# A job list that counts DMA transfers one behind the other, three matmuls less at the start of banks, and a new order of splits under the last A V product

## The chip, the core and the metric

The kernel runs on one core of a Trainium2 chip. The metric is device time in microseconds (us) of one launch. The core has five engines, each of which takes its own instructions in program order: PE (TensorE: matrix products into the eight PSUM banks), DVE (VectorE), ACT (ScalarE), POOL (GpSimd) and SP (SyncE, which here does little but issue DMA transfers). They meet only through semaphores, so an instruction that waits holds up all that stands behind it on its engine.

## The reference, cut to what matters

```python
# q, k, v: (4, 12, 448, 64) float32
scores = np.matmul(q, k.transpose(0, 1, 3, 2)) / np.sqrt(64)     # causal mask, softmax over the last axis
x = np.matmul(softmax(scores), v)                                 # -> (4 * 448, 12 * 64) = (1792, 768)
h = x @ w_in                                                      # w_in (768, 2048)
g = np.maximum(h, 0.0) + alpha * np.minimum(h, 0.0)               # PReLU, alpha per column
out = g @ w_out                                                   # w_out (2048, 768) -> (1792, 768)
```

The two weight matrices arrive as 64-bit floats; the kernel makes 32-bit floats of them with integer operations on their halves.

## The kernel before, in words

**Attention.** The 24 pairs of heads (six for each of four batches) go through a software pipeline. A text table (`ORDER`) says for every round which step of which pair is emitted: scores (`S0`..`S2`), row maxima, exponentials, normalising on POOL (`NO`), transposes on PE (`PT`, L582), their copies out of PSUM (`C00`, `C10`, `C21`, ...: DVE L504, ACT L502), and the product with V (`AV`, L602). Other work hangs on steps of single pairs by hooks (`after(pair, step, function)`).

**Both layers of the MLP** are block products with seven products in place of eight. The steps are called P1, P5, P6, P2, P7, P3, P4; each reads one block or sum of blocks of the left side (A11, S1, S2, A12, S3, S4, A22) and one of the right side (B11, T1, T2, B21, T3, B22, T4) and writes a bank in the role Y, V, X or Z. After P1, ACT copies bank Y to bank X (`fork`; L402 in the first layer, L1371 in the second). After P5, ACT copies bank V to SBUF (`keep`; L406, L1376). After P6 DVE or ACT makes bank Z from Y and the kept V (`Z`, L409; `oz` in the second layer, L1383 or L1275), and P7 and P3 wait for that. Each operand is split into a high and a low part: ACT rounds a copy (the cast, "hi"), DVE or POOL subtracts it from the operand ("lo"), and PE multiplies hi by hi, lo by hi and hi by lo. A step therefore waits for the "lo" of both its operands.

**First layer.** `h_step` (matmuls on L395, nine of 128x448 to a step) runs groups g = 0..7 of `w_in`, for the two halves b = 0, 1 of the tokens. Group 0 of half 0 runs between the last steps of attention. Half 1 needs the splits of its x blocks T1, T2, T3, T4, B21, B22 (ACT `x2_hi`, L849; DVE `x2_lo`, L853). B22 and two thirds of B21 come back from DRAM by DMA (`x2l_B<-xd_B`); the last third of B21 and T4 are what the last `AV` completes. `FIRST` is the order of the steps of group 0 for half 1. The results go through ACT `relu` (L419), DVE `act` (L423) and a store (L429) to DRAM (`gd`). A "piece" is 768 KB of a 64-bit weight matrix: loaded by SP (L278, L283), then ACT L296 and L300, POOL L304, DVE L308 and L312, POOL L318; pieces of `w_out` are stored to DRAM (`wd`, L323).

**Second layer.** Four quarters Q of `w_out`, each for seven row tiles, are 28 tiles q, taken in 14 pairs p; a step is six matmuls of 128x384 (L1262). For every pair SP loads g (`gl`, four transfers on L1210), and sums (L1230), casts (ACT L1236) and lows (L1240) follow. For every quarter SP loads weights (`wl`, L1178), and sums (DVE L1188), casts (ACT L1195, into a slot `w`) and lows (DVE L1199) follow. The quarter changes inside pair 3 (tile 6 is of quarter 0, tile 7 of quarter 1).

**What sets the order.** From the end of attention on, everything is a job of `Plan`. A job names its engine, a duration (table `US`), the jobs it comes after, the room (a buffer slot) that it takes and the ones it gives back, and a due time, which is worked back from the order of the steps on PE. `Plan.order` plays the list through when the program is built, starting on each idle engine the ready job with the earliest due time, and the instructions are emitted in the order of these starts. So the model of time in `Plan` sets only an order; on the chip each engine keeps that order and waits as it must. `busy["way"]` keeps POOL and the marked DVE operations from overlapping in the plan. In the kernel before, a load counts as landed 4.0 us after its issue and a store 3.0 us, however many others are under way.

`ready_bank` takes the next PSUM bank and runs one matmul of 128x448 on it (L803) whose result nothing uses.

## Time and profile before

| what | value |
|---|---|
| median of 3 runs | 586.35 us (584.92 to 589.84) |
| profiled execution | 589.1 us, its span 587.3 us, so 1.8 us around the span |
| PE busy | 572.3 us, 97% of the span |
| DVE, ACT, POOL busy | 473.6 (81%), 390.0 (66%), 294.0 us (50%) |
| mean granted clock of PE | 0.993 |
| chain that ended last | 84% PE, 7% DVE, 4% DMA |

Span is from the first to the last instruction of the profiled execution. A busy share is the time in which an engine had an instruction under way. The granted clock is a share of full speed: 1.0 is 2.4 GHz and 0.5 is 1.2 GHz. The chain that ended last is followed back from the last instruction to what released each one. In a timeline, the bracket at the end of a line is the idle time of the engine just ahead of it and what ended it. "x1l", "gset" and so on in the rows are buffers; "bank" is any PSUM bank.

### The profile page before, as it was taken

The numbers are of one execution on the slowest core, as the hardware profiler recorded it, in microseconds if no ns is written. First come the engines' busy times: TensorE is split into PE (matmuls) and PEld (weight loads), VectorE is DVE, ScalarE is ACT, GpSimd is POOL, SyncE is SP. The second block draws the span as 40 slices with busy tenths as digits, with TensorE's granted clock in tenths as the row PEclk, the third lists the DMA queues.
The fourth block names the chain that finished last, engine by engine and source line by source line (L and its number), as shares of the span: only waits on it lengthen the run. The fifth ranks groups of instructions, "written<-read, shape, count | busy, mean of one in ns | idle before, by whom it ended". The sixth has DMA issues, their size and how long they took to land.

```text
span 587.3 us, 10245 instructions
## 1 busy us (share of the span) xinstructions
PE 572.3 (97%) x3300; PEld 498.2 (85%) x3300; DVE 473.6 (81%) x993; ACT 390.0 (66%) x898; POOL 294.0 (50%) x340
## 2 busy tenths in 40 slices
PE   8999999999998999999999999989989999999997
PEld 4666676666877999999999998989879999999997
DVE  5998998899779687687678779858989888879963
ACT  6989897999676566665656636667756656555431
POOL 7766687875624433544445414224525552645530
PEclk9999999999998999999999999989999999999999
DMA  6876546321336575766767564873352414403532
GB/s 167 211 149 172 136 127 178 113 65 63 89 139 217 182 252 203 255 221 222 266 216 251 166 216 148 262 239 127 99 153 77 140 42 148 133 10 119 179 108 108
DMA packets 82981, 93.48 MB, mean 159 GB/s; under 512 B 11632, under 2 KB 72016, under 8 KB 82928
## 3 DMA queue, kind: packets, MB, share of 16 engines
q1 hardware_dynamic: 82032, 91.19, 49.8%
q0 software_dynamic: 576, 1.18, 0.8%
q8 instruction: 26, 0.43, 0.3%
q10 hardware_dynamic: 320, 0.46, 0.3%
q14 instruction: 27, 0.22, 0.1%
HBM read 64.50 MB, written 28.31 MB: 158 GB/s over the span
## 4 chain that ended last, share of the span: by engine, by line
PE 84%; DVE 7%; DMA 4%; issue 2%; ACT 2%; SPq 1%; POOL 0%; DVEq 0%; ACTq 0%; POOLq 0%
PE bank L395 31%; PE bank L1262 27%; PE bank L602 8%; PE bank L582 7%; PE bank L525 6%; PE bank L517 4%; DMA tf<-gd 2%; DMA gd<-tf 2%; DVE dec L1188 1%; DVE x1l L1240 1%; DVE x1h L1199 1%; PE bank L445 1%; DVE tf L423 1%; SPq L1210 0%; DMA wd<-acc 0%
## 5 line engine op out<-in xcount | busy, mean ns | idle before, releaser
L506 POOL TENSOR_SCALAR p<-p,rs 128x128 f32<-128x128 f32 (+3 forms) x164 | 84.3, 533 | 34.9 <-DVE rs L563 17.1
L552 ACT ACTIVATE p<-bank,nm 128x256 f32<-128x256 f32 (+3 forms) x168 | 82.5, 507 | 14.0 <-DVE nm L537 11.2
L1262 PE MATMUL bank<-x1h,x1l 128*128 128x384 f32 x444 | 81.9, 335 | 1.3 <-DVE x1h L1199 1.3
L1262 PEld LDWEIGHTS bank<-x1h,x1l 128*128 128x128 f32 x444 | 77.8, 188 | 1.6 <-DVE x1h L1199 1.5
L537 DVE CUSTOM_DVE_ANT_0 bank<-bank,mask 128x128 f32<-128x128 f32 (+3 forms) x168 | 71.0, 480 | 9.7 <-PE bank L525 5.6
L419 ACT ACTIVATE tf<-bank 128x448 f32<-128x448 f32 x64 | 34.1, 542 | 35.0 <-PE bank L395 21.3
L582 PEld LDWEIGHTS bank<-ident,p 128*128 128x128 f32 x384 | 43.3, 141 | 12.0 <-issue 7.8
L423 DVE SCALAR_TENSOR_TENSOR tf<-tf,om,bank 128x448 f32<-128x448 f32 x64 | 41.4, 673 | 13.3 <-ACT tf L419 13.2
L602 PEld LDWEIGHTS bank<-ptf,v 128*64 128x64 f32 x384 | 25.4, 136 | 30.8 <-issue 13.0
L582 PE MATMUL bank<-ident,p 128*128 128x128 f32 x384 | 47.2, 274 | 0.9 <-POOL p L506 0.8
L1262 PE MATMUL bank<-x1h,gset 128*128 128x384 f32 x228 | 45.1, 348 | 2.5 <-ACT bank L1371 1.8
L602 PE MATMUL bank<-ptf,v 128*64 128x448 f32 (+3 forms) x384 | 46.8, 386 | 0.0
L395 PE MATMUL bank<-x1h,wir 128*128 128x448 f32 x192 | 44.7, 368 | 0.5 <-DVE bank L409 0.5
L1262 PEld LDWEIGHTS bank<-x1h,gset 128*128 128x128 f32 x228 | 41.5, 195 | 3.4 <-ACT bank L1371 2.2
L318 POOL TENSOR_TENSOR dec<-dec,tf 128x768 int32<-128x768 int32 x13 | 26.3, 2020 | 33.4 <-ACT tf L419 13.7
L525 PE MATMUL bank<-kr,qr 64*128 64x384 f32 (+2 forms) x288 | 41.0, 397 | 0.0
L395 PEld LDWEIGHTS bank<-x1h,wir 128*128 128x128 f32 x192 | 35.9, 188 | 4.1 <-DVE bank L409 0.8
L502 ACT ACTIVATE ptf<-bank 128x512 f32<-128x512 f32 (+1 forms) x71 | 38.0, 583 | 1.7 <-PE bank L582 1.7
L1262 PE MATMUL bank<-wo,x1l 128*128 128x384 f32 x186 | 35.7, 339 | 1.1 <-DVE wo L1199 1.1
L552 ACT ACTIVATION_READ_ACCUMULATOR p<-bank,nm 128x1 f32 x168 | 35.9, 214 | 0.0
L1262 PEld LDWEIGHTS bank<-wo,x1l 128*128 128x128 f32 x186 | 32.9, 188 | 1.5 <-DVE wo L1199 1.5
L409 DVE TENSOR_TENSOR bank<-bank,tf 128x448 f32<-128x448 f32 x30 | 18.9, 629 | 18.6 <-PE bank L395 18.4
(190 smaller groups left out, 1383.2 us busy)
## 6 DMA issues: line engine op xcount, KB each, us to landing
gd<-tf SPq DMA_DIRECT2D x64, 224.0 KB, 2.0
tf<-gd SPq DMA_DIRECT2D x28, 256.0 KB, 4.4
acc<-gd SPq DMA_DIRECT2D x28, 256.0 KB, 4.4
dec<-in_moe_w_in_dram SPq DMA_DIRECT2D x9, 768.0 KB, 4.9
tf<-in_moe_w_in_dram SPq DMA_DIRECT2D x7, 768.0 KB, 4.6
dec<-in_moe_w_out_dram SPq DMA_DIRECT2D x7, 768.0 KB, 5.0
tf<-in_moe_w_out_dram SPq DMA_DIRECT2D x7, 768.0 KB, 4.3
dec<-wd SPq DMA_DIRECT2D x13, 384.0 KB, 4.5
```

The source lines that it names most:

```text
L318: nc.gpsimd.tensor_tensor(out=y, in0=y, in1=low, op=ALU.add)
L395: nc.tensor.matmul(ps, w[:, u, k * P : (k + 1) * P], x[:, k], start=(st in ("P1", "P5") and i == 0), stop=(i == len(mms) - 1), skip_group_ ...
L419: nc.scalar.activation(t, bank_of(g, b, role), AF.Relu, scale=-1.0)
L423: stt(out=t, in0=t, scalar=om[:, f : f + 1], in1=bank_of(g, b, role), op0=ALU.mult, op1=ALU.add)
L502: eng.activation(out, x, AF.Copy, scale=side)
L506: eng.tensor_scalar(out=out, in0=x, scalar1=side, scalar2=1.0, op0=ALU.mult, op1=ALU.mult)
L525: nc.tensor.matmul(ps[:, o : o + lim], T["q", p][half(j), i * QP : (i + 1) * QP], T["k", p][half(j), :lim], start=(o == 0), stop=(n > 0 or ...
L537: nc.vector.tensor_tensor_reduce(out=t, in0=t, in1=masks[1] if i == NQ else masks[0][:, (NQ - 1 - i) * QP :], scale=-SCALE, scalar=MOST_F3 ...
L552: nc.scalar.activation(T["p", p, i][:, j, : t.shape[1]], t, AF.Exp, scale=-1.0, bias=T.pop(("nm", p, i, j)), accum_out=T["sm", p][:, z : z ...
L582: nc.tensor.transpose(ps[:, j - js[0], c], t[:, j, c * QP : (c + 1) * QP], T["ident"])
L602: nc.tensor.matmul(out[half(j), c * QP :], vs[b % 2][:, hp, c, j], x[:, c * QP : S], start=(c == 0), stop=(c == NQ),)
L1262: nc.tensor.matmul(ps, x, w, start=(st in ("P1", "P5")[: 1 if Q else 2] and i == 0), stop=(i == len(mms) - 1), skip_group_check=True,)
```

## The change

- `Plan` knows a transfer's length (`move`, table `MOVE`): a transfer lands at the later of its issue plus 1.35 and the landing of the one before it, plus its own length. Loads with a due time are not issued earlier than 45 us ahead of it.
- Three of the four `ready_bank` matmuls go; the banks are taken as they are.
- `Z` of group 0, half 0, is hooked behind the copy `C00` instead of `C21` of the last pair, so it stands one copy earlier on DVE.
- T3's cast is emitted behind T1's and T2's, ahead of the last `AV`'s results; it is no job any more.
- In group 0 of half 1, P2 (which reads B21) runs ahead of P7 (T3) and P3 (B22); B21 is loaded ahead of B22.
- The casts of quarter weights keep the order of the steps (`wc_last`).

Left out of the diff: the parameter `move` itself, handed down by the other jobs that issue a transfer.

```diff
--- before.py
+++ after.py
@@ -60,13 +60,17 @@
...
+START, AHEAD = 1.35, 45.0
+MOVE = {"raw": 2.7, "piece": 1.4, "x": 0.9, "act": 0.62, "w": 0.95, "g": 1.05, "out": 0.7}
...
@@ -102,7 +106,9 @@
...
-        busy, events, now = {}, [], 0.0
+        busy, now, moved = {}, 0.0, 0.0
+        early = dict(then=[], next=[], give=[], n=-1)
+        events = [(j["by"] - AHEAD, 0, early) for j in self.jobs if j["move"] and AHEAD < j["by"] < 1e6]
...
@@ -119,6 +125,8 @@
...
+                    if j["move"] and j["lag"] == LOAD and now < j["by"] - AHEAD - 1e-6:
+                        continue
...
@@ -127,7 +135,10 @@
...
-                    events += [(now + us, 0, j), (now + us + j["lag"], 1, j)]
+                    end = now + us + j["lag"]
+                    if j["move"]:
+                        end = moved = max(moved, now + START) + j["move"]
+                    events += [(now + us, 0, j), (end, 1, j)]
...
@@ -170,7 +181,7 @@
...
 STEPS = ["P1", "P5", "P6", "P2", "P7", "P3", "P4"]
-FIRST = ["P1", "P5", "P6", "P7", "P3", "P2", "P4"]
+FIRST = ["P1", "P5", "P6", "P2", "P7", "P3", "P4"]
...
@@ -804,8 +815,7 @@
...
     def begin_block():
-        y, v_, x = ring.popleft(), ring.popleft(), ready_bank()
-        bk[0] = [y, v_, x, None]
+        bk[0] = [ring.popleft() for _ in range(3)]
         rooms["v"] = Slots([ap["low"].tile([P, S], F32, tag="low", name="low_v")])
         for st in ("P1", "P5"):
...
@@ -817,7 +827,7 @@
...
     def plus_z():
-        bk[0][3] = ready_bank()
+        bk[0].append(ring.popleft())
         h_plus(0, 0, "Z")
 
...
@@ -855,7 +865,7 @@
     def scores_over():
...
-        for nm in ("T1", "T2"):
+        for nm in ("T1", "T2", "T3"):
             x2_hi(nm, (0, KW))
...
@@ -908,7 +918,7 @@
...
         after(last - 1, "AV", go_on)
-        after(last, "C21", plus_z)
+        after(last, "C00", plus_z)
         after(last, "C30", last_of_it)
...
@@ -922,15 +932,15 @@
...
-        bk[1] = [ready_bank(), ready_bank(), ring.popleft(), ring.popleft()]
-        bk[1] = bk[1][2:] + bk[1][:2]
+        v_, z, y, x = ring.popleft(), ready_bank(), ring.popleft(), ring.popleft()
+        bk[1] = [y, v_, x, z]
...
-        done.add(("load", piece_names[3]))
+        done |= {("load", piece_names[3]), ("xh", "T3")}
...
@@ -980,7 +990,7 @@
...
-        PARTS = {"T3": (0, KW), "B22": (0, KW), "B21": (0, KW - 1), "T4": (0, KW)}
+        PARTS = {"T3": (0, KW), "B21": (0, KW - 1), "B22": (0, KW), "T4": (0, KW)}
...
@@ -989,11 +999,12 @@
...
-                job(("xh", nm), "ACT", f"cast{n}", lambda nm=nm, ks=ks: x2_hi(nm, ks), of)
+                if ("xh", nm) not in done:
+                    job(("xh", nm), "ACT", f"cast{n}", lambda nm=nm, ks=ks: x2_hi(nm, ks), of)
...
@@ -1287,7 +1298,7 @@
...
-                    dec_end + [("store", ("o", 4 * Q + c + 2 * u)) for u in range(2)], "wf", lag=LOAD, behind=list(wl_last),
+                    dec_end + [("store", ("o", 4 * Q + c + 2 * u)) for u in range(2)], "wf", lag=LOAD, behind=list(wl_last), move=MOVE["w"],
...
@@ -1308,7 +1319,8 @@
...
-                job(("wcast", Q, nm), "ACT", "wcast", lambda nm=nm: w_cast(Q, nm), of, "w")
+                job(("wcast", Q, nm), "ACT", "wcast", lambda nm=nm: w_cast(Q, nm), of, "w", behind=list(wc_last))
+                wc_last[:] = [("wcast", Q, nm)]
...
@@ -1322,7 +1334,7 @@
...
-                        lag=LOAD, behind=gl_last + ([] if first else [("gl", 2 * p, 0)]),
+                        lag=LOAD, move=MOVE["g"], behind=gl_last + ([] if first else [("gl", 2 * p, 0)]),
...
```

The new file is longer, so its lines have other numbers: what was L402, L406, L409, L419, L849, L853 is L413, L417, L420, L430, L859, L863, and what was L296, L1178, L1188, L1199, L1210, L1240 is L307, L1189, L1199, L1210, L1221, L1251.

ACT at the end of attention, before (`x2h_T` and `x2h_B` are casts of x blocks of half 1, `dec<-dec` a piece, L402 the fork and L406 the keep of half 1):

```order
L849 ACTIVATE x2h_T_2343<-tf 128x1344
L502 ACTIVATE x2h_B_2370<-bank_65 128x448
L849 ACTIVATE x2h_T_2345<-tf 128x1344
L296 ACTIVATE dec<-dec 128x768
L300 ACTIVATE dec<-dec 128x768
L849 ACTIVATE x2h_T_2366<-tf 128x1344
L402 ACTIVATE bank_64<-bank_68 128x448
L849 ACTIVATE x2h_B_2368<-x2l_B_2369 128x1344
L406 ACTIVATE tf<-bank_65 128x448
L849 ACTIVATE x2h_B_2370<-x2l_B_2371 128x896
L373 ACTIVATE wie<-dec 128x384
L419 ACTIVATE tf<-bank_63 128x448
```

and now:

```order
L859 ACTIVATE x2h_T_2341<-tf 128x1344
L859 ACTIVATE x2h_T_2343<-tf 128x1344
L513 ACTIVATE x2h_B_2369<-bank_65 128x448
L307 ACTIVATE dec<-dec 128x768
L311 ACTIVATE dec<-dec 128x768
L859 ACTIVATE x2h_T_2365<-tf 128x1344
L430 ACTIVATE tf<-bank_63 128x448
L859 ACTIVATE x2h_B_2369<-x2l_B_2370 128x896
L413 ACTIVATE bank_65<-bank_68 128x448
L384 ACTIVATE wie<-dec 128x384
L430 ACTIVATE tf<-bank_67 128x448
L417 ACTIVATE tf<-bank_64 128x448
```

T3's cast is third of three at the start; the cast of B21 (128x896) stands ahead of the fork (now L413), which stood ahead of both casts of B blocks; the cast of B22 comes behind the keep.

SP at the beginning of the second layer, before (`gd_87<-tf` stores the last results of the first layer, `acc<-gd` and `tf<-gd` load g for the pairs 1 and 2, `in_moe_w_out` is a piece):

```order
L1178 DMA wie<-wd 128x2x384
L429 DMA gd_87<-tf 128x448
L1178 DMA dec<-wd 128x2x384
L429 DMA gd_87<-tf 128x448
L1178 DMA dec<-wd 128x2x384
L283 DMA tf<-in_moe_w_out_dram 128x1536
L1210 DMA tf<-gd_84 128x4x128 x4
L1178 DMA dec<-wd 128x2x384
L323 DMA wd<-acc 128x768
```

and now:

```order
L1189 DMA wie<-wd 128x2x384
L440 DMA gd_87<-tf 128x448 x2
L1189 DMA dec<-wd 128x2x384
L440 DMA gd_87<-tf 128x448
L1221 DMA tf<-gd_84 128x4x128 x4
L1189 DMA dec<-wd 128x2x384 x2
L294 DMA tf<-in_moe_w_out_dram 128x1536
L334 DMA wd<-acc 128x768
L294 DMA acc<-in_moe_w_out_dram 128x1536
```

The load of g for pair 2 stood behind a piece and now stands ahead of it. On ACT, at the same place, before (L296 and L300 are that piece, L1236 casts of g, L1371 the forks of tiles 2 and 3):

```order
L296 ACTIVATE tf<-tf 128x768
L300 ACTIVATE tf<-tf 128x768
L1236 ACTIVATE x1l<-acc 128x512
L1371 ACTIVATE bank_62<-bank_63 128x384
L1236 ACTIVATE x1l<-acc 128x512
L1371 ACTIVATE bank_61<-bank_65 128x384
L1236 ACTIVATE x1l<-tf 128x512
L1376 ACTIVATE acc<-bank_67 128x384
```

and now:

```order
L1383 ACTIVATE bank_62<-bank_63 128x384
L1247 ACTIVATE x1l<-acc 128x512
L1383 ACTIVATE bank_61<-bank_64 128x384
L1247 ACTIVATE x1l<-tf 128x512
L1388 ACTIVATE acc<-bank_67 128x384
L1247 ACTIVATE x1l<-tf 128x512
L1388 ACTIVATE acc<-bank_65 128x384
L1247 ACTIVATE x1l<-tf 128x512
L1395 ACTIVATE bank_66<-bank_63 128x384
L1247 ACTIVATE x1l<-acc 128x512
L307 ACTIVATE tf<-tf 128x768
L1395 ACTIVATE bank_68<-bank_64 128x384
L311 ACTIVATE tf<-tf 128x768
```

Both forks (now L1383) are ahead of the piece (now L307 and L311), which stands between the two `oz` of tiles 2 and 3 (now L1395).

DVE at the change from quarter 0 to quarter 1, before (L1188 sums and L1199 lows of the weights, L1230 sums and L1240 lows of g, L1275 the fork of tile 7):

```order
L1188 TENSOR_TENSOR dec<-dec,wie 128x768
L1199 TENSOR_TENSOR wie<-wie 128x2x384
L1240 TENSOR_TENSOR x1l<-dec,x1l 128x512
L1199 TENSOR_TENSOR wo<-dec,wo 128x2x384
L1240 TENSOR_TENSOR x1l<-dec,x1l 128x512
L1188 TENSOR_TENSOR dec<-dec 128x768
L1230 TENSOR_TENSOR acc<-acc 128x512
L1275 TENSOR_TENSOR bank_65<-bank_61,acc 128x384
L1397 COPY acc<-bank_67 128x384
L1397 COPY tf<-bank_64 128x384
L1199 TENSOR_TENSOR x1h<-dec,x1h 128x2x384
```

and now:

```order
L1199 TENSOR_TENSOR dec<-dec,wie 128x768
L1210 TENSOR_TENSOR wie<-wie 128x2x384
L1241 TENSOR_TENSOR dec<-dec,acc 128x512
L1251 TENSOR_TENSOR x1l<-dec,x1l 128x512
L1210 TENSOR_TENSOR wo<-dec,wo 128x2x384
L1251 TENSOR_TENSOR x1l<-dec,x1l 128x512
L1199 TENSOR_TENSOR dec<-dec 128x768
L1241 TENSOR_TENSOR acc<-acc 128x512
L1286 TENSOR_TENSOR bank_64<-bank_61,acc 128x384
L1409 COPY acc<-bank_67 128x384
L1409 COPY tf<-bank_65 128x384
L1210 TENSOR_TENSOR wo<-dec,wo 128x2x384
```

The low of T2 (the last row of each) went to a slot in `x1h`, which quarter 0 still used, and now goes to `wo`; one sum of g more (now L1241) is done on DVE.

## Rows read from the trace of the kernel before

**Rows 1.** Timeline of PE, 162 to 188 us: start, length, idle before.
```profile
162.58 1.50 PE L395 MATMUL bank<-x1h,wir 128*128 128x448 f32 x6 [0.54 <-DVE bank L409]
...
168.35 0.68 PE L803 MATMUL bank<-x1h,wie 128*128 128x448 f32 x2
...
172.56 1.40 PE L395 MATMUL bank<-x2h_T,wie 128*128 128x448 f32 x6
...
174.41 1.39 PE L395 MATMUL bank<-x2h_T,wie 128*128 128x448 f32 x6
...
178.28 1.67 PE L395 MATMUL bank<-x2h_T,wir 128*128 128x448 f32 x6 [1.87 <-DVE bank L409]
...
180.86 2.30 PE L395 MATMUL bank<-x2h_B,wir 128*128 128x448 f32 x6
...
187.29 1.39 PE L395 MATMUL bank<-x1h,wie 128*128 128x448 f32 x6
```

**Rows 2.** Busy us by stretch, then the granted clock.
```profile
180.00:182.00 2.00, 2.00 (x7) 1.76 (x7) 1.89 (x3) 2.00 (x4) 0.83 (x1) 0.50 1.13 217
...
420.00:440.00 20.00, 16.47 (x89) 14.91 (x88) 17.79 (x25) 11.87 (x22) 5.91 (x4) 1.00 0.38 113
```

**Rows 3.** Timeline of DVE from 176 to 180 us.
```profile
176.14 1.55 DVE L853 TENSOR_TENSOR x2l_B<-x2l_B,x2h_B 128x1344 fp32r<-128x1344 f32 x1
177.60 0.62 DVE L409 TENSOR_TENSOR bank<-bank,tf 128x448 f32<-128x448 f32 x1
178.14 1.85 DVE L423 SCALAR_TENSOR_TENSOR tf<-tf,om,bank 128x448 f32<-128x448 f32 x3
```

**Rows 4.** Timeline of PE from 363 to 400 us.
```profile
363.78 1.49 PE L395 MATMUL bank<-x2h_T,wir 128*128 128x448 f32 x6 [1.45 <-DVE bank L409]
...
383.99 4.33 PE L1262 MATMUL bank<-x1h,gset 128*128 128x384 f32 x24
390.15 6.00 PE L1262 MATMUL bank<-x1h,gset 128*128 128x384 f32 x24 [1.83 <-ACT bank L1371]
```

**Rows 5.** Timeline of DVE from 361 to 424 us.
```profile
361.14 2.04 DVE L1188 TENSOR_TENSOR dec<-dec 128x768 f32<-128x768 f32 x1
363.11 0.62 DVE L409 TENSOR_TENSOR bank<-bank,tf 128x448 f32<-128x448 f32 x1
...
414.71 2.05 DVE L1199 TENSOR_TENSOR wie<-wie 128x768 fp32r<-128x768 f32 x1
...
422.71 0.94 DVE L1199 TENSOR_TENSOR x1h<-dec,x1h 128x768 fp32r<-128x768 f32 x1
```

**Rows 6.** The chain that ended last: start, length, what.
```profile
349.08 5.82 DMA tf<-gd
...
373.64 9.33 DMA gd<-tf
```

**Rows 7.** Timeline of ACT from 387 to 391 us.
```profile
387.52 0.90 ACT L296 ACTIVATE tf<-tf 128x768 f32<-128x768 f32 x1 [3.60 <-DMA tf<-in_moe_w_out_dram]
...
389.63 0.47 ACT L1371 ACTIVATE bank<-bank 128x384 f32<-128x384 f32 x1
```

**Rows 8.** Timeline of ACT from 169 to 177 us.
```profile
169.63 1.32 ACT L849 ACTIVATE x2h_T<-tf 128x1344 fp32r<-128x1344 f32 x1
170.85 0.90 ACT L296 ACTIVATE dec<-dec 128x768 f32<-128x768 f32 x1
...
173.66 0.53 ACT L402 ACTIVATE bank<-bank 128x448 f32<-128x448 f32 x1
...
175.76 0.94 ACT L849 ACTIVATE x2h_B<-x2l_B 128x896 fp32r<-128x896 f32 x1
```

**Rows 9.** Timeline of SP's queue at 168 us.
```profile
168.50 0.80 SPq L992 DMA_DIRECT2D x2l_B<-xd_B  x2
```

**Rows 10.** DMA issues, 150 to 200 us: KB, us to landing.
```profile
x2l_B<-xd_B SPq DMA_DIRECT2D x1, 672.0 KB, 4.0
...
x2l_B<-xd_B SPq DMA_DIRECT2D x1, 448.0 KB, 4.7
```

More of the change, by code (lines that the diff above doesn't have):

```diff
@@ L67, in __init__, with job @@
         self.room, self.jobs, self.named, self.done = dict(room), [], {}, set(done)
-    def job(self, name, eng, kind, fn, after=(), take="", give=(), lag=0.2, by=1e9, behind=()):
+    def job(self, name, eng, kind, fn, after=(), take="", give=(), lag=0.2, by=1e9, behind=(), move=0.0):
         deps = []
@@ L76, in job @@
             name=name, eng=eng, us=US[kind], fn=fn, on=eng, left=len(deps) + len(first), after=deps, then=[], next=[], take=take, give=list(give),
-            lag=lag, by=by, at=None, n=len(self.jobs), shared=kind in SHARED,
+            lag=lag, by=by, at=None, n=len(self.jobs), shared=kind in SHARED, move=move,
         )
@@ L942, in piece_jobs @@
             if ("load", key) not in done:
-                job(("load", key), "SP", "issue", lambda: p_load(key), of, room_of(key, "raw"), lag=LOAD, by=by, behind=[("load", before)])
+                job(("load", key), "SP", "issue", lambda: p_load(key), of, room_of(key, "raw"), lag=LOAD, by=by, behind=[("load", before)], move=MOVE["raw"])
             if ("abs", key) not in done:
@@ L951, in piece_jobs @@
             if key[0] == "o":
-                job(("store", key), "SP", "issue", lambda: p_store(key), [("add", key)], give=[room_of(key, "y")], lag=STORE, by=by)
+                job(("store", key), "SP", "issue", lambda: p_store(key), [("add", key)], give=[room_of(key, "y")], lag=STORE, by=by, move=MOVE["piece"])
         def add_of(g, nm):
@@ L991, in x2_jobs @@
                         ("xl", nm), "SP", "issue",
-                        lambda nm=nm, part=part: nc.sync.dma_start(out=x32(nm)[:, part], in_=xd[nm][:, part]), lag=LOAD,
+                        lambda nm=nm, part=part: nc.sync.dma_start(out=x32(nm)[:, part], in_=xd[nm][:, part]), lag=LOAD, move=MOVE["x"] * ks[1],
                     )
@@ L1020, in act @@
                 job(("act", g, b, role), "DVE", "act", lambda: h_act(g, b, role), [("relu", g, b, role)])
-                job(("st", g, b, role), "SP", "issue", lambda: h_store(g, b, role), [("act", g, b, role)], give=["t"], lag=STORE)
+                job(("st", g, b, role), "SP", "issue", lambda: h_store(g, b, role), [("act", g, b, role)], give=["t"], lag=STORE, move=MOVE["act"])
             me = ("P", g, b, st)
@@ L1078 @@
                     job(("act", 0, 0, role), "DVE", "act", lambda role=role: h_act(0, 0, role), [("relu", 0, 0, role)])
-                    job(("st", 0, 0, role), "SP", "issue", lambda role=role: h_store(0, 0, role), [("act", 0, 0, role)], give=["t"], lag=STORE)
+                    job(("st", 0, 0, role), "SP", "issue", lambda role=role: h_store(0, 0, role), [("act", 0, 0, role)], give=["t"], lag=STORE, move=MOVE["act"])
             for b, st in turns:
@@ L1409, in o_jobs @@
                 of, i, n, z = ends[st]
-                job(("out", q, st), "SP", "issue", lambda: o_out(q, n, z, a[i], nc.sync), [(of, q)], lag=STORE)
-        wl_last, begun = [], set()
+                job(("out", q, st), "SP", "issue", lambda: o_out(q, n, z, a[i], nc.sync), [(of, q)], lag=STORE, move=MOVE["out"])
+        wl_last, wc_last, begun = [], [], set()
         class At:
```

## The prediction

> **What bounds the kernel now.** I read the page first. PE is busy 97% of the span and the chain that ended last is 84% PE, so the kernel takes as long as PE's matmuls do, plus the places where PE waits or runs at half clock. Everything that a new order of the other engines can give lies in those places. The stretches of the span show three of them. I then read PE's timeline in each for the idle time and its releaser, and from there the releasing engine's timeline.
>
> The first is the end of attention. PE waits 0.54 and then 1.87 us for DVE's Z [rows 1]. Behind the second wait the granted clock is 0.50, that is 1.2 GHz [rows 2]: six matmuls take 2.30 us there and 1.39 us later [rows 1]. The reader is to see why Z is late: it stands on DVE directly behind the low of B22, 1.55 us long [rows 3], though P7, which needs it, needs no B22.
>
> The second is the change from the first layer to the second. At 363.78 PE has waited 1.45 us and at 390.15 1.83 us [rows 4]. The first wait again ends with Z, started behind a weight sum of 2.04 us at 361.14 [rows 5]; the whole row of DVE work was late because g landed 5.82 us after its last issue [rows 6], where the job list counted 4.0. The second ends with a fork that ACT ran at 389.63, behind a piece that it had waited 3.60 us for [rows 7]. That piece could only be issued when a store had landed, 9.33 us after its issue [rows 6], where the list counted 3.0. Half clock follows here too: 24 matmuls take 6.00 us behind the wait and 4.33 us ahead of it [rows 4].
>
> The third is the change to quarter 1: PE is busy 16.47 of the 20 us from 420 on, so 3.53 us are lost, at full clock, while DVE is busy 17.79 us [rows 2].
>
> Between these places, from 180 to 345 us and from 440 us on, PE never waits. Idle time of the other engines there is worth nothing.
>
> **The change, part by part.** One step of the first layer on PE is 174.41 - 172.56 = 1.85 us [rows 1].
>
> *Three matmuls less.* Two of them are 0.68 us with the tail of the second [rows 1], so 0.34 each at most, and nothing if PE waited anyway. I take 0.25, near the upper end, because PE works back to back at two of the three: 0.75 us.
>
> *Z one copy earlier.* The wait of 0.54 goes [rows 1] up to a few hundredths of semaphore; I take 0.45, between 0 and 0.54. So the last AV ends 0.95 us earlier (two of the matmuls lie ahead of it), and P5 of half 1 1.2 us earlier, at 174.41 - 1.2 = 173.2.
>
> *The splits.* T3's cast costs ACT 170.85 - 169.63 = 1.22 us [rows 8] in the tight stretch behind AV; now it lies ahead, where ACT waited for AV. Ahead of the fork come now a relu, 0.45 us (the fork's own kind and size, 0.53 with its tail), and B21's cast, 0.94 with its tail, 0.83 without [rows 8]. So the fork moves from 173.66 to 173.66 - 0.95 - 1.22 + 0.45 + 0.83 = 172.8 and ends at 173.3, if B21 has landed by 171.9. P6 waits for it 0.1 us, to 173.3. P6 and P2 take PE to 177.0. Z needs P6 (175.2) and DVE, where it now has the low of B21 ahead of it (two thirds of 1.55, so 1.0 [rows 3]), a low of 0.5 and one act of 0.6 (three are 1.85 [rows 3]): 176.14 - 0.95 + 1.0 + 0.5 + 0.6 = 177.3 at the latest, if nothing of the earlier cast comes through on DVE, and 176.1 if all of it does. I take 176.6, so P7 does not wait. What is late next is B22: its cast now follows the keep and ends at 175.9, and its low stands behind Z and two acts: 176.6 + 0.6 + 1.2 + 1.5 = 179.4 with semaphores, where P7 is done at 178.9. So P3 waits 0.4 us. No wait as long as 1.87 is left, and at 162.58 a wait of 0.54 was followed by no slow matmuls [rows 1]; so the half clock goes: P7, P3, P2 and P4 took 187.29 - 178.28 = 9.01 us where four steps are 7.40 [rows 1], so 1.61 us. In all 0.75 + 0.45 + 1.87 + 1.61 - 0.1 - 0.4 = **4.2 us**, between 2.5 (half clock comes back) and 4.7 (no new wait).
>
> B21's landing is the open price. Both loads were issued from 168.50 on [rows 9], when that AV was done, B22 landed 4.0 us after its issue as the first and B21 4.7 us as the second [rows 10]. Issued 0.95 us earlier, B21 lands between 171.5 and 172.3, and the fork may be 0.4 us later than above. I take no delay, because B21, the smaller, is now the first; both ends are in the range. The Trainium skill ("DMA: Bandwidth & Descriptors", Anatomy of one DMA) fits 2.0 us plus the bytes at 436 GB/s, which makes 3.1 us of 448 KB (an estimate); by that the cast would never wait and the sum would be the same, but both measured landings are longer.
>
> *Landings one behind the other, at the first change of layers.* DVE's rows for the second layer are now ordered for later landings: Z of half 1 follows the sum T2 at a place where the loads are expected late. The wait of **1.45 us** goes; between 0 and 1.45, and I take all of it, because every DVE job ahead of that Z is now one that the plan itself puts behind the landing.
>
> *The forks ahead of the piece.* Both forks now stand ahead of the piece on ACT, and pair 2's g ahead of it on SP, so 1.83 goes and with it 6.00 - 4.33 = 1.67 of half clock [rows 4]: **3.5 us**. What is late next: the piece's first operation now stands ahead of tile 3's `oz`. The piece was there at 387.52 [rows 7]. The four transfers of g now ahead of it take up to 5.8 us [rows 6], so it comes between 387.5 and 393.3; with 0.9 for the operation and 0.5 for `oz` [rows 7] that is 388.9 to 394.7. P7 of tile 3 is nine steps behind the P1 at 383.99; four steps are 4.33 with a tail, so 1.04 each [rows 4], and it is due at 393.4. So 0 to 1.3 us come back; I take **0.6**.
>
> *Weight casts in the order of the steps.* At the change to quarter 1, T2's low no longer waits for a slot that quarter 0 still uses. But DVE had no gap there, and the lost time was mostly lows such as the one of 2.05 us, where the same operation takes 0.94 elsewhere [rows 5]: 1.1 us for each that meets POOL. In the new order POOL holds fewer jobs of pair 3 and DVE more sums. I count two such meetings, 2.2 us late, less some 0.9 us of slack that the low of T2 has, plus 0.2 of smaller waits: 1.5 of the 3.53 stay, so **2.0 us** go, between 0 and 3.53.
>
> *Elsewhere.* The pieces and stores of groups 1 to 7 are reordered too. PE had no wait there, so there is nothing to win; I put in 0.6 us of new waits, between 0 and 3.
>
> Sum: 589.1 - 4.2 - 1.45 - 3.5 - 2.0 + 0.6 + 0.6 = 579.15, so **579 us**. The profiled execution lies 2.75 us above the median of the runs, 586.35; since what I take away are mostly its waits, I do not take these 2.75 off again, and let the range reach lower instead.
>
> **The rivals.**
>
> *Nothing comes back.* The third place goes too, the piece is in time, no new wait: 589.1 - 4.2 - 1.45 - 3.5 - 3.53 = 576.4 us. For it speaks that DVE, ACT and POOL have slack everywhere else; against it DVE's 17.79 of 20 us there. Chance 0.20.
>
> *Waits move instead of going.* The piece comes at its late end (1.3 us) and half clock follows (1.67), and quarter 1 loses its 3.53 as before: 589.1 - 4.2 - 1.45 - 3.5 + 3.0 = 583 us. For it: nothing in the change gives DVE less to do. Against it: at 363.78 a wait of 1.45 us brought no slow matmuls [rows 4]. Chance 0.27.
>
> *Slower: DVE meets POOL at the changes of quarters.* Each change brings 11 sums and lows of weights on DVE, now packed in step order into the pair in which the quarter changes. Each that meets POOL costs 1.1 us [rows 5]. It happens at pair 3 and again at pair 10, where the kernel before had no wait. If seven of 11 meet at each, less 0.9 of slack, the loss is 6.8 us at each, 10.1 more than before: 589.1 - 9.15 + 10.1 = 590; with all 11 some 599. From seven on it is slower than before. Against it speaks that the plan still keeps the two engines apart, and that at pair 10 the same 11 operations made PE wait nowhere before. Chance 0.08, around 594. The Trainium skill ("GPSIMD Reference", Key points) says that GpSimd shares its SBUF interfaces with VectorE and contends with operations of two SBUF inputs. By that rule any of these sums and lows can be hit; the trace agrees where it can be seen, 2.05 us against 0.94.
>
> **How the numbers follow.** My forecast, 577 to 581.5 with its own bounds, has 0.45. The range of 8 in 10 runs from 574.5 (nothing comes back, and part of the 2.75 with it) to 585.5 (moved waits, with one more in the groups). A difference of 1%, 5.9 us, is about what a measurement of this kernel can tell from none; so faster means below 580.5 and slower above 592.2. Faster: 0.85 of the forecast and the first rival, 0.38 + 0.20 = 0.58. Same: the rest of the forecast, the second rival and a little of the third, 0.35. Slower: 0.07.
>
> **What would show it.** In the profile after: no PE wait over 1 us before 190 us, and the granted clock at 1.0 there; from the first matmul of `ready_bank` behind the last AV to group 1 it was 187.29 - 168.35 = 18.9 us [rows 1] and would be 15.7, 3.2 less, since 0.95 of the 4.2 lie ahead of it. No wait of PE for ACT's fork in pair 1, and Z of group 7, half 1, done before P2 ends. A wait of PE for `oz` of tile 3 would show the piece late; lows of 2 us on DVE beside POOL at the change to quarter 1 would show that its loss stays. I am wrong if PE waits at new places between 190 and 345 us, or if half clock appears behind waits shorter than those of before.

## The result, and the profile after

The changed kernel takes **577.47 us** (median of 6 runs, 577.27 to 578.48), the kernel before 586.92 us in the runs beside it (6 runs, 584.92 to 589.84): a ratio of 0.984 (95% interval 0.982 to 0.987), 9.5 us or 1.6% less. The prediction was 579.0 us, in a range of 574.5 to 585.5, with a chance of 0.58 for faster by over 1%. One run among all of those below, of the kernel b1, took 621.37 us at a mean granted clock of 0.851 and is left out of the figures. The profiled execution of the changed kernel took 577.39 us, with a span of 575.6, 11.7 us less than that of before; PE is busy 567.6 us, 99% of it, and its mean granted clock is 1.0.

The timeline of PE at the end of attention (start, length, what, idle before in brackets), to be held against [rows 1]:

```profile
161.90 1.50 PE L406 MATMUL bank<-x1h,wir 128*128 128x448 f32 x6
...
167.67 0.47 PE L814 MATMUL bank<-x1h,wie 128*128 128x448 f32 x1
...
175.57 1.38 PE L406 MATMUL bank<-x2h_B,wir 128*128 128x448 f32 x6
...
177.45 1.50 PE L406 MATMUL bank<-x2h_T,wir 128*128 128x448 f32 x6
...
183.06 1.18 PE L406 MATMUL bank<-x1h,wie 128*128 128x448 f32 x5
```

No line carries a bracket: the waits of 0.54 and 1.87 us are gone, P7 starts at 177.45, and group 1 at 183.06 where it started at 187.29 [rows 1], 4.2 us earlier. From the remaining `ready_bank` matmul to group 1 it is 15.4 us. DVE's timeline there shows why:

```profile
173.84 1.08 DVE L863 TENSOR_TENSOR x2l_B<-x2l_B,x2h_B 128x896 fp32r<-128x896 f32 x1
...
176.77 0.63 DVE L420 TENSOR_TENSOR bank<-bank,tf 128x448 f32<-128x448 f32 x1
177.30 1.26 DVE L434 SCALAR_TENSOR_TENSOR tf<-tf,om,bank 128x448 f32<-128x448 f32 x2
178.48 1.56 DVE L863 TENSOR_TENSOR x2l_B<-x2l_B,x2h_B 128x1344 fp32r<-128x1344 f32 x1
```

The low of B21 runs first, Z (L420) ends at 177.4, and the long low of B22 stands behind it, not ahead as in [rows 3]. B21 landed 3.4 us after its issue and B22 4.7:

```profile
x2l_B<-xd_B SPq DMA_DIRECT2D x1, 672.0 KB, 4.7
...
x2l_B<-xd_B SPq DMA_DIRECT2D x1, 448.0 KB, 3.4
```

At the change of layers PE has no wait either (timeline of PE, then of ACT; compare [rows 4] and [rows 7]):

```profile
361.63 1.38 PE L406 MATMUL bank<-x2h_T,wir 128*128 128x448 f32 x6
...
378.03 8.49 PE L1273 MATMUL bank<-x1h,gset 128*128 128x384 f32 x48
386.36 4.34 PE L1273 MATMUL bank<-x1h,x1l 128*128 128x384 f32 x24
```

```profile
379.33 0.47 ACT L1383 ACTIVATE bank<-bank 128x384 f32<-128x384 f32 x1 [0.64 <-PE bank L1273]
...
380.37 0.47 ACT L1383 ACTIVATE bank<-bank 128x384 f32<-128x384 f32 x1
...
385.02 0.91 ACT L307 ACTIVATE tf<-tf 128x768 f32<-128x768 f32 x1 [0.58 <-DMA tf<-in_moe_w_out_dram]
385.84 0.48 ACT L1395 ACTIVATE bank<-bank 128x384 f32<-128x384 f32 x1
```

The 48 matmuls that were 24, a wait, and 24 at half clock are one line of 8.49 us. The first fork (L1383) waits for PE, the second follows a cast of g at once; neither stands behind the piece any more. The piece (L307) still waits for its transfer, but now tile 3's `oz` alone stands behind it, and that ends at 386.3, a step before it is due at about 387.4 (nine steps of 1.04 behind 378.03). The transfers did not get faster: between 360 and 400 us the stores of the first layer land after 7.9 us and pair 2's g after 8.0 us, where the same views of the kernel before have 2.0 and 5.9.

The DMA issues of the changed kernel, 360 to 400 us (KB, median us to landing):

```profile
tf<-gd SPq DMA_DIRECT2D x4, 256.0 KB, 8.0
gd<-tf SPq DMA_DIRECT2D x4, 224.0 KB, 7.9
```

All that PE still loses behind its start lies at the change to quarter 1 (PE, then DVE, then POOL):

```profile
413.07 1.15 PE L1273 MATMUL bank<-wo,x1l 128*128 128x384 f32 x5 [0.28 <-DVE wo L1210]
...
420.85 1.15 PE L1273 MATMUL bank<-x1h,x1l 128*128 128x384 f32 x5 [0.87 <-DVE x1h L1210]
...
423.98 1.29 PE L1273 MATMUL bank<-x1h,gset 128*128 128x384 f32 x6 [0.93 <-DVE acc L1286]
```

```profile
417.88 0.95 DVE L1199 TENSOR_TENSOR dec<-dec 128x768 f32<-128x768 f32 x1
418.75 2.05 DVE L1210 TENSOR_TENSOR x1h<-dec,x1h 128x768 fp32r<-128x768 f32 x1
420.72 1.77 DVE L1241 TENSOR_TENSOR dec<-tf 128x512 f32<-128x512 f32 x1
```

```profile
416.13 1.84 POOL L1251 TENSOR_TENSOR x1l<-acc,x1l 128x512 fp32r<-128x512 f32 x1 [12.74 <-ACT x1l L1247]
417.94 2.04 POOL L1251 TENSOR_TENSOR x1l<-tf,x1l 128x512 fp32r<-128x512 f32 x1
419.95 2.00 POOL L1251 TENSOR_TENSOR gset<-tf,gset 128x512 fp32r<-128x512 f32 x1
```

2.1 us of waits are left where 3.5 were [rows 2]. On DVE a low of 2.05 us and a sum of 1.77 us run beside two lows of POOL, the sign that the prediction named for a loss that stays.

### The profile page after: what moved, and what is told of

Read it like the earlier page. It is cut to its first block, busy times and chain, and to the rows that moved or that the text cites. A ratio compares the mean times of both kernels' runs of the same rounds, so it can differ in the third digit from the quotient of the medians.

```text
span 575.6 us, 10260 instructions
## 1 busy us (share of the span) xinstructions
PE 567.6 (99%) x3297; PEld 494.9 (86%) x3297; DVE 469.3 (82%) x998; ACT 389.7 (68%) x898; POOL 287.7 (50%) x335
## 4 chain that ended last, share of the span: by engine, by line
PE 95%; DVE 3%; issue 1%; ACT 0%; POOL 0%; DVEq 0%; POOLq 0%
PE bank L406 36%; PE bank L1273 32%; PE bank L613 8%; PE bank L593 8%; PE bank L536 6%; PE bank L528 4%; PE bank L456 1%; DVE x1l L1251 1%; DVE x1h L1210 0%; DVE dec L1199 0%; DVE dec L1241 0%; DVE wo L1210 0%; DVE bank L548 0%; ACT p L563 0%; DVE wie L1210 0%
## 5 line engine op out<-in xcount | busy, mean ns | idle before, releaser
L1273 PE MATMUL bank<-x1h,x1l 128*128 128x384 f32 x540 | 98.7, 336 | 1.0 <-DVE x1h L1210 0.9
L1273 PEld LDWEIGHTS bank<-x1h,x1l 128*128 128x128 f32 x540 | 94.3, 188 | 1.6 <-DVE x1h L1210 1.2
L430 ACT ACTIVATE tf<-bank 128x448 f32<-128x448 f32 x64 | 34.3, 543 | 40.4 <-PE bank L406 29.9
L406 PE MATMUL bank<-x1h,wir 128*128 128x448 f32 x192 | 44.7, 368 | 0.0
L1273 PE MATMUL bank<-x1h,gset 128*128 128x384 f32 x216 | 40.4, 338 | 0.9 <-DVE acc L1286 0.9
L1273 PEld LDWEIGHTS bank<-x1h,gset 128*128 128x128 f32 x216 | 37.9, 188 | 1.2 <-ACT acc L1407 1.2
L406 PEld LDWEIGHTS bank<-x1h,wir 128*128 128x128 f32 x192 | 36.0, 188 | 3.3
L329 POOL TENSOR_TENSOR dec<-dec,tf 128x768 int32<-128x768 int32 x11 | 22.1, 2009 | 30.9 <-ACT tf L430 16.4
L420 DVE TENSOR_TENSOR bank<-bank,tf 128x448 f32<-128x448 f32 x30 | 18.9, 631 | 22.2 <-PE bank L406 18.3
L1251 POOL TENSOR_TENSOR x1l<-acc,x1l 128x512 fp32r<-128x512 f32 x12 | 16.4, 1365 | 40.7 <-ACT x1l L1247 31.7
L406 PE MATMUL bank<-x1h,wie 128*128 128x448 f32 x144 | 33.4, 367 | 0.0
```

Source lines behind the costliest of these rows:

```text
L406: nc.tensor.matmul(ps, w[:, u, k * P : (k + 1) * P], x[:, k], start=(st in ("P1", "P5") and i == 0), stop=(i == len(mms) - 1), skip_group_ ...
L430: nc.scalar.activation(t, bank_of(g, b, role), AF.Relu, scale=-1.0)
L1273: nc.tensor.matmul(ps, x, w, start=(st in ("P1", "P5")[: 1 if Q else 2] and i == 0), stop=(i == len(mms) - 1), skip_group_check=True,)
```

## The experiments

Times are medians; e0 to e3 ran on one chip (the kernel before there 587.29 us), a0 to a3 on another (586.21 us), b1 to b3 on another (587.86 us), c1 by itself (587.10 us). The kernel before differs by up to 1.7 us from chip to chip, so a smaller difference between runs of two chips says little.

**The spread of the kernel before (e0).** No edit.

> The kernel before, run again for its spread. Its profiled execution was 589.1 us, its runs lie between 584.9 and 589.8, those of the changed kernel between 577.3 and 578.5. If the half clock behind the waits is what differs between executions, the mean granted clock goes down as the time goes up: about 0.999 at 585 us, 0.993 at 589 us, with 1.2 us for each slow stretch of six matmuls less or more. If the clock is 0.993 in all of them, the spread comes from the lengths of the waits themselves.

Measured: 586.92 us (583.77 to 591.02). Of the 33 runs in that comparison, the six with a mean clock of 0.999 or 1.0 have a median of 585.0 us, the ten at 0.993 or 0.994 one of 589.0, the 13 at 0.997 one of 587.0 and the four at 0.996 one of 587.5. So the time goes with the clock, at about its full size: 0.007 of 587 us are 4.1. The clock is not all of it: at 0.997 the runs still lie between 585.2 and 591.0. This execution's change of layers on PE:

```profile
364.13 1.49 PE L395 MATMUL bank<-x2h_T,wir 128*128 128x448 f32 x6 [1.84 <-DVE bank L409]
...
390.32 4.43 PE L1262 MATMUL bank<-x1h,gset 128*128 128x384 f32 x24 [1.63 <-ACT bank L1371]
```

Waits of 1.84 and 1.63 us, and full clock behind both: the 24 matmuls take 4.43 us, not 6.00 [rows 4]. The execution that the prediction was built on had one slow stretch more than this one, worth 6.00 - 4.43 = 1.6 us and not the 1.2 expected. Its other slow stretch, behind the 1.87 us at the end of attention, is here too.

**The end of attention alone (e1).** The kernel before with these edits only:

```diff
-FIRST = ["P1", "P5", "P6", "P7", "P3", "P2", "P4"]
+FIRST = ["P1", "P5", "P6", "P2", "P7", "P3", "P4"]
...
```

Left out of this cut: Z at `C00`, T3's cast early, B21 ahead of B22, and three `ready_bank()` that become `ring.popleft()`, all as in the change.

> The kernel before with the edits at the end of attention alone: three ready_bank matmuls out, Z hooked behind C00, T3's cast early, P2 ahead of P7 and P3, B21 loaded ahead of B22. The job list counts transfers as before. Theory (the wait for Z came from the low of B22 ahead of it on DVE, and the half clock from the wait): 4.2 us less than the kernel before, about 582.7 us, no PE wait over 1 us ahead of 190 us, and the waits of 1.45 and 1.83 us at the change of layers and the 3.5 us at quarter 1 still there. Rival (the job list's landings are what moved Z and the lows): the 1.87 us wait and the half clock stay, only 1.2 us go, about 585.7 us.

Measured: 586.69 us (585.0 to 588.7; ratio 0.999, 0.997 to 1.001). Both theories fall: the wait of 1.87 us is gone, and yet nothing is gained. PE's timeline:

```profile
177.69 0.88 PE L395 MATMUL bank<-x2l_B,wir 128*128 128x448 f32 x3 [1.08 <-DVE x2l_B L852]
...
183.26 1.49 PE L395 MATMUL bank<-x2h_T,wir 128*128 128x448 f32 x6 [1.03 <-DVE bank L409]
...
185.21 1.39 PE L395 MATMUL bank<-x1h,wie 128*128 128x448 f32 x6
...
389.32 6.93 PE L1262 MATMUL bank<-x1h,gset 128*128 128x384 f32 x24 [4.39 <-ACT bank L1371]
```

Two waits of 1 us take the place of the old one, so group 1 starts at 185.21, 2.1 us earlier than before and not 4.2. The wait of 1.45 us for group 7's Z is gone too, so the second layer starts 3.4 us earlier (366.01, from 369.41). Then all of it is given back at the fork of pair 1: 4.39 us of wait, and 6.93 us for 24 matmuls that take 4.33 at full clock. ACT, the chain of waits and the DMA issues of this kernel show why:

```profile
385.80 0.89 ACT L296 ACTIVATE tf<-tf 128x768 f32<-128x768 f32 x1 [6.15 <-issue]
...
388.79 0.48 ACT L1371 ACTIVATE bank<-bank 128x384 f32<-128x384 f32 x1
```

```profile
370.97 9.21 DMA gd<-tf
```

```profile
tf<-in_moe_w_out_dram SPq DMA_DIRECT2D x1, 768.0 KB, 5.5
```

The piece's load goes out at 380.26, when a store has landed that took 9.21 us, and lands 5.5 us later, at 385.8, where ACT has waited for it. PE reaches the fork 3.4 us earlier than before, but the piece comes only 1.7 us earlier and the fork 0.8 (388.79, from 389.63 [rows 7]), so PE waits for the difference.

DVE explains the first 2.1 us:

```profile
174.57 1.27 DVE L423 SCALAR_TENSOR_TENSOR tf<-tf,om,bank 128x448 f32<-128x448 f32 x2
175.75 0.63 DVE L409 TENSOR_TENSOR bank<-bank,tf 128x448 f32<-128x448 f32 x1
176.29 2.81 DVE L852 TENSOR_TENSOR x2l_B<-x2l_B,x2h_B 128x896 fp32r<-128x896 f32 x2
```

With 4.0 us for any load the list puts two acts and Z ahead of B21's low, and P2 waits for that low. With the new landings it comes first.

**The landings alone (e2).** The changed kernel with the end of attention and the casts' order of before.

> The kernel before with the job list's landings alone (START, AHEAD, MOVE); the end of attention and the order of the weight casts are as before. Theory: the waits of 1.45 and 1.83 us and the half clock behind the second go, 5.0 us less, about 581.9 us; the wait for Z of 1.87 us ahead of 190 us and its half clock stay, and at quarter 1 about 3.5 us stay. Rival (landings do all of it): 578.7 us, with the wait for Z gone too.

Measured: 581.44 us (580.9 to 583.2; ratio 0.989, 0.986 to 0.993). The theory holds, by 0.5 us. The waits of the change of layers are gone, and this one stays:

```profile
178.68 2.01 PE L406 MATMUL bank<-x2h_T,wir 128*128 128x448 f32 x6 [1.87 <-DVE bank L420]
...
187.66 1.39 PE L406 MATMUL bank<-x1h,wie 128*128 128x448 f32 x6
```

From P7 to group 1 it takes 8.98 us where four steps are 7.40: the half clock, 1.6 us, as in [rows 1]. This profiled execution took 582.9 us at a mean clock of 0.997. Four of the six runs, at a clock of 1.0, took 580.9 to 581.5, so they had no such stretch, and the median is theirs: the half clock that the theory kept is not in it. At quarter 1 the waits sum to 3.1 us.

So the parts do not add up from the kernel before: the end alone is worth 0.2 to 0.6 us, which is not clear of nothing, the landings alone 5.5 to 5.9, all of the change 9.5. On top of the landings the end's edits (with the casts) are worth 3.5 to 4.

**The end and the forks (b3).** The kernel e1 with an order by hand in the list, and the old landings:

```diff
+late = [("abs", ("o", 14))] + [("gcast", 2, nm) for nm in LEFT] + [("wcast", 1, nm) for nm in OPS]
+for j in late:
+    pl.wait_issue(pl.named[j], [("ofork", 3)])
+pl.wait_issue(pl.named["load", ("o", 14)], [("gl", 5, 1)])
```

> The kernel with the edits at the end of attention alone (landings 4.0 and 3.0 us as before), and one order by hand: at the change of layers the piece, pair 2's casts and quarter 1's casts stand behind both forks of pair 1 on ACT, and pair 2's four loads of g ahead of the piece's load on SP. Theory (what the end of attention won was waited away at that fork, 4.4 us with 2.6 us of slow matmuls behind it, because the piece's landing is set by the stores ahead of it and not by PE): 5 to 7 us less than with the edits at the end alone, 579.7 to 581.7 us. Rival (the wait goes to the next work that needs a late transfer, pair 2's g): at most 2 us less, 584.7 us or more, and a wait of PE for x1l or gset between 385 and 410 us.

Measured: 580.67 us (579.5 to 584.3; ratio 0.988, 0.984 to 0.992), 6.0 less than e1, as the theory has it. PE, then ACT:

```profile
380.59 8.49 PE L1262 MATMUL bank<-x1h,gset 128*128 128x384 f32 x48
389.31 4.43 PE L1262 MATMUL bank<-x1h,x1l 128*128 128x384 f32 x24 [0.23 <-ACT bank L1383]
```

```profile
381.89 0.47 ACT L1371 ACTIVATE bank<-bank 128x384 f32<-128x384 f32 x1 [1.12 <-PE bank L1262]
...
386.14 0.89 ACT L296 ACTIVATE tf<-tf 128x768 f32<-128x768 f32 x1 [2.74 <-DMA tf<-in_moe_w_out_dram]
```

The piece comes no earlier (386.14, in e1 385.80). The forks no longer stand behind it, and 4.39 + 2.60 us become 0.23. So the place of the forks is the cause of the lost gain in e1, and this order by hand, which moves pair 2's loads and casts too, gives 6.0 of the 9.2 us that lie between e1 and the changed kernel; some 2.1 of the rest are the end of attention, where group 1 starts at 185.16 here.

**Longer constants (b2).** The changed kernel without the rule of one transfer behind the other:

```diff
-LOAD, STORE = 4.0, 3.0
+LOAD, STORE = 5.8, 6.0
...
-                    if j["move"]:
-                        end = moved = max(moved, now + START) + j["move"]
```

> The changed kernel with two longer constants in place of the transfers one behind the other: a load lands 5.8 us after its issue and a store 6.0 us, however many are under way; all else as changed. Theory (the list must know which transfers are crowded, and a constant puts the lone ones too late): waits of over 1 us come back, 579 to 583 us. Rival (any later landing puts the forks and Z ahead): within 0.7 us of the changed kernel, 577.5 us.

Measured: 590.04 us (588.8 to 590.6; ratio 1.004, 1.002 to 1.006), worse than either theory. Behind its start PE waits at eleven places, 10.4 us in sum, three of them:

```profile
178.87 0.88 PE L404 MATMUL bank<-x2l_B,wir 128*128 128x448 f32 x3 [1.77 <-DVE x2l_B L861]
...
294.35 0.47 PE L404 MATMUL bank<-x1h,wir 128*128 128x448 f32 x1 [0.79 <-ACT wir L382]
...
346.24 1.29 PE L404 MATMUL bank<-x1h,wir 128*128 128x448 f32 x5 [1.03 <-DVE wir L386]
```

The last two lie between 190 and 350 us, where PE waits in no other kernel here. So these two longer constants do not do in place of the rule. That it is the transfers that are alone which suffer by them, as the theory has it, is not shown apart.

**Without the casts' order (e3).** The changed kernel without `wc_last`.

> The changed kernel without the order of the weight casts (wc_last). Theory (the casts' order is what saved 1.4 us at quarter 1): 578.9 us, T2's low again written to a slot of x1h, 3.5 us lost between 400 and 440 us. Rival (what is lost at quarter 1 is set by how many sums and lows of DVE meet POOL, whatever the order of the casts): within 0.5 us of the changed kernel, 577.5 us.

Measured: 578.04 us (577.5 to 579.0), 0.1 us above the changed kernel's second median (a0) and 0.6 above its first. PE waits 1.56 and 1.17 us for lows at quarter 1, 2.7 us in all and not 3.5. DVE there:

```profile
412.83 2.04 DVE L1199 TENSOR_TENSOR dec<-dec 128x768 f32<-128x768 f32 x1
414.80 2.03 DVE L1210 TENSOR_TENSOR wo<-dec,wo 128x768 fp32r<-128x768 f32 x1
```

T2's low goes to a slot of `x1h` again (at 411.95), as the theory has it, but that costs next to nothing. The rival is the nearer: as in the changed kernel, two operations of DVE run beside lows of POOL (1.54 us at 412.52 and 1.99 at 414.02).

**The changed kernel again (a0).**

> The changed kernel again, as the mark for the runs beside it on the same chip: 577.5 us, between 577.2 and 578.6 as before.

Measured: 577.91 us (577.45 to 578.15). Its waits at quarter 1 are 0.82, 0.91 and 0.93 us, 2.7 in sum; the 2.1 above was a short one.

**The three matmuls back (a1).**

```diff
-        bk[0] = [ring.popleft() for _ in range(3)]
+        bk[0] = [ring.popleft(), ring.popleft(), ready_bank()]
-        bk[0].append(ring.popleft())
+        bk[0].append(ready_bank())
-        v_, z, y, x = ring.popleft(), ready_bank(), ring.popleft(), ring.popleft()
+        v_, z, y, x = ready_bank(), ready_bank(), ring.popleft(), ring.popleft()
```

> The changed kernel with the three ready_bank matmuls put back at their three places, and nothing else. Theory (each costs 0.25 us of PE's time): 0.75 us more than the changed kernel. Rival (they stood where PE had a wait ahead or behind anyway, or they overlap): 0 to 0.2 us more.

Measured: 578.55 us (578.15 to 580.5), 0.64 more than a0; group 1 starts at 183.67, where it is 183.14 in a0. The theory holds for the size of the sum, a little under 0.25 each; one of the three brings a wait of 0.29 us for Z with it (at 162.52), so not all of it is matmul.

**The old order of steps (a2).** The changed kernel with `FIRST` and `PARTS` of before.

> The changed kernel with group 0 of half 1 in the old order (P7 and P3 ahead of P2) and B22 loaded and split ahead of B21; the list's landings stay. The list puts Z ahead of the lows of B22 and B21 on DVE here, behind two acts. Theory (P7 comes one step too early for a Z that waits for P6, its act and its place): Z ends near 176.7 us where P7 is due at 175.6, a wait of about 1.2 us, no slow matmuls or 1.6 us of them, so 1.2 to 2.8 us more than the changed kernel. Rival (the landings alone put Z in time, the order of the steps is worth nothing): within 0.3 us of the changed kernel.

Measured: 578.48 us (578.0 to 579.7), 0.57 more than a0.

```profile
176.81 1.49 PE L406 MATMUL bank<-x2h_T,wir 128*128 128x448 f32 x6 [1.05 <-DVE bank L420]
...
184.24 1.39 PE L406 MATMUL bank<-x1h,wie 128*128 128x448 f32 x6
```

The wait came as the theory has it, 1.05 us at full clock, and group 1 starts 1.1 us later than in a0. The time lies between theory and rival: at quarter 1 the first wait is 0.24 us here and 0.82 in a0. But it was 0.28 in the first profile of the changed kernel, so it is not shown that the old order of steps makes up half there.

**Quarter 1 (a3, c1, b1).** a3 holds pair 4's first work back; c1 holds its low of A22 back as well:

```diff
+("glo", p, nm), "DVE" if p == 4 and nm in ("A11", "A12") else "DVE|POOL", ...
+pl.wait_issue(pl.named["gsum", 4, "S1"], [("w22", 7)])
+for nm in ("A11", "A12"):
+    pl.wait_issue(pl.named["glo", 4, nm], [("w22", 7)])
+pl.wait_issue(pl.named["glo", 4, "A22"], [("glo", 4, "S3")])      # c1 alone
```

> The changed kernel with pair 4's first work held back at quarter 1: its lows of A11 and A12 are done by DVE in place of POOL, and these and its first sum stand behind the copy of bank Y of tile 7's P7 on DVE. Theory (the 0.87 us wait there is a low of 2.05 us that met POOL's two lows, and the 0.93 us wait comes from the sum of 1.77 us ahead of that copy): both waits go, 1.3 to 1.8 us less than the changed kernel, lows of 0.95 us at that place. Rival (DVE is full there, whatever meets POOL; what is taken off the one wait comes back at pair 4's own lows): within 0.4 us of the changed kernel, with a wait of PE for pair 4's x1l or gset.

Measured: 577.29 us (576.6 to 577.6), 0.62 less than a0, between the theories. The wait of 0.93 us for the copy of bank Y is gone; that of 0.92 us stays, behind a DVE low of 2.06 us (at 419.28) that ran beside a POOL low of 2.06 (at 418.46).

> The kernel with pair 4's first work held back at quarter 1, and one order more: pair 4's low of A22 stands behind its low of S3 on POOL, where it cannot run before pair 4's sums; the copies of bank Y stay where they were. Theory (the low of B22 on DVE took 2.06 us and made PE wait 0.92 us because it ran beside POOL's low of A22): that low takes 0.95 us, the wait goes, 576.3 to 576.6 us. Rival (DVE is full there and PE only waits elsewhere): 577 us or more, with a wait of about the same size at the next lows.

Measured: **576.65 us** (576.42 to 576.89; ratio to the kernel before 0.982, 0.979 to 0.985), below every run of the changed kernel. DVE, then POOL, then PE:

```profile
418.53 0.95 DVE L1210 TENSOR_TENSOR x1h<-dec,x1h 128x768 fp32r<-128x768 f32 x1
```

```profile
425.81 1.30 POOL L1251 TENSOR_TENSOR x1l<-acc,x1l 128x512 fp32r<-128x512 f32 x1 [8.04 <-ACT x1l L1247]
```

```profile
412.86 1.14 PE L1273 MATMUL bank<-wo,x1l 128*128 128x384 f32 x5 [0.24 <-DVE wo L1210]
...
434.46 4.09 PE L1273 MATMUL bank<-x1h,x1l 128*128 128x384 f32 x22 [0.86 <-DVE x1l L1251]
```

The same low, at the same place on DVE, takes 0.95 us once POOL runs nothing beside it (idle for the 8.04 us up to 425.81), and both waits of 0.9 us are gone. That much of the theory is shown; of the rival a part is true too, since 0.86 us come back 15 us later at a low of pair 4.

> The kernel with pair 4's first work held back at quarter 1, and two orders more: pair 4's low of A22 stands behind its low of S2 on POOL, and the copies of bank Y of tiles 4 and 5 stand behind T2's low on DVE. Theory (the 2.05 us low met POOL's low of A22; T2's low waited 0.9 us for the two copies ahead of it): the waits of 0.9 and of 0.3 to 0.8 us for lows of quarter 1 go as well, 575.5 to 576 us. Rival (DVE is full there): the same lows are late again, 577 us or more.

Measured: 576.9 to 578.7 us in five runs, with 577.6 in the middle, no better than a3, so its theory falls. What the further order of POOL and the moved copies each cost was not separated, so why it is no better than a3 stays open.

## Why the prediction was right, and where not

**The end of attention: 4.2 us, right in size, wrong in cause.** The trace lost 4.23 us there, and a1, a2 and e2 show the parts: 0.6 for the three matmuls (0.75 forecast), a wait of 1.05 us that P2's place ahead of P7 avoids, and, where only the landings change, a wait of 1.87 us that stays, with 1.6 us of half clock in the profiled execution. But the forecast put all of it down to the edits there. "Z needs P6 (175.2) and DVE, where it now has the low of B21 ahead of it" was read from the new order and is right, yet that order needs the new landings: without them (e1) B21's low stands behind Z, and half of the 4.2 is lost on the spot. The waits of 0.1 us for the fork and 0.4 us for B22 did not come to more than some 0.1 each. That the sum meets 4.23 so closely is in part luck: at P6 of half 1 (173.62, from 174.41) PE is 0.8 us ahead where 1.1 was forecast, and behind it PE wins 3.4 where 3.1 was.

**Z of group 7: 1.45 us, right in size, its cause only in part.** From group 1 to the second layer it took 182.12 us before and takes 180.40 now, 1.7 less; a wait costs PE slightly more than its bracket. The landings alone do it (e2), as forecast, but they are not needed: in e1, with the old landings, the wait is gone too. Z stands behind the weight sum there as before, but that sum starts at 357.10 and not at 361.14 [rows 5]; ahead of it two lows take 0.68 us each where the kernel before has 1.47 and 1.79.

**The forks: 3.5 us, right in mechanism, too large for a usual run.** Wait and slow matmuls are gone, by the order that b3 tests alone. But the 1.67 us of half clock, a part of this term, were not in e0's profile, and the clocks fit two slow stretches in only ten of the 33 runs. The two of the profiled execution, 3.3 us, are more than the 0.003 of 587 us, 1.8, that the run in the middle of the kernel before has. This is most of why the traces differ by 11.7 us and the medians by 9.5. Not to take the 2.75 us off again was right all the same: the slow stretches went with the waits, and the profiled execution after, 577.39, lies at its median.

**Quarter 1: 2.0 us, met by one pair of traces, wrong in cause.** From the 133rd matmul of the second layer (395.99 and 386.36) to the end of the span it took 191.3 us before and 189.2 after, 2.1 less, but 0.7 less between the second executions, e0 and a0. The waits there are 3.5 and 3.1 us in two executions before, 2.1 and 2.7 after. The step that failed is "weight casts in the order of the steps": without it the time is the same within 0.1 to 0.6 us (e3), and e1 and b3, which have neither that order nor the new landings, wait 1.7 and 2.1 us there, no more than the changed kernel (e1 behind its long wait at the fork, b3 with an order by hand). So other changes of the list move these waits as much, and where 2.0 was met, it was by luck. What sets them is what the same paragraph named second, DVE's lows beside POOL (c1); its count of two meetings was right. The list keeps the two apart in its own time, but on the chip POOL's lows begin when ACT's cast is done, as at 416.13 behind 12.74 us of idle time.

**The two charges, 0.6 + 0.6 us, did not come.** The piece came in the middle of its range (385.02, which is 390.97 in the time of the kernel before, as the second layer starts 5.95 us earlier), a step ahead of the due `oz`. From 183 to 400 us PE waits nowhere. They are most of what the forecast missed: it took 10.0 us off the profiled execution, and 11.7 came off, 4.2 at the end of attention, 1.7 at group 7, 3.7 at the forks and 2.1 behind them, with no charge of 1.2. So 579 stands beside 577.5. That 10.0 lies near the 9.5 of the medians is chance, since the profiled execution before was 2.2 us slower than its median.

**The rivals.** "Nothing comes back" was nearest, 576.4. "Slower" did not happen; its mechanism did, at two operations of the change in pair 3 and not seven, and at others later (a low of 2.05 us at 458.32) where PE waits for none. "Waits move" is what the change's one half does alone (e1).

## What to carry to other kernels

A place where an engine waits behind a late transfer can take back all that is won ahead of it, as in e1: find the next such place down the program before an earlier gain is counted, and move what does not need the transfer ahead of it. A list that counts transfers one behind the other paid here, by 5.5 to 5.9 us alone; two longer constants for all in its place made the changed kernel 12 us slower. And a sum made from one profiled execution gives the time after, not the difference of the medians: the clocks of the other runs tell what that execution had and they had not.

## What the hardware showed beside that

Half clock does not follow every wait of a size. It came behind 1.87 us in three executions (before, e0, e2), behind 1.77 (b2, where the granted clock is 0.60 from 180 to 184 us) and behind 4.39, and not behind 1.05 and 1.08, nor behind 1.56 and 1.17 at quarter 1 (e3). Between them it is open: behind the same fork 24 matmuls took 6.00 us after a wait of 1.83 [rows 4], and 4.43 after one of 1.63 (e0), where a wait of 1.84 us brought none either.

A DVE low of 0.95 us took 2.05 beside POOL, and POOL's own took 2.04 where one by itself takes 1.29 (at 426.54). The Trainium skill ("SBUF — State Buffer", SBUF: two separate sides) has it that whichever of the two starts first holds the shared ports for its whole instruction. The trace agrees: the DVE sum of 0.95 us, begun at 417.88, just ahead of that POOL low, lost nothing; the POOL low ends 1.15 us after the sum, and DVE's low, begun while it ran, 0.82 us after the POOL low. The times are as if each waited for the other and then took about its own time.
